# A gated mix of sliding-window attention and a GELU MLP on one core: the account of dense products per score step, weighted by stage

## The chip, the cores and the metric

One core of one Trainium2 chip. The metric is the device time of one launch in microseconds (us), the median of several runs. A profile of one launch goes with it; its span runs from the first to the last instruction on the core. The engines are named as the profile names them: PE (matrix products; PEld is its weight load), DVE (vector engine), ACT (scalar engine), POOL (GpSimd) and SP (the queue that issues the DMAs here).

## The reference, cut to what matters

x is 2048 x 512. Two branches are mixed by a gate per row: attention with 32 heads of width 16 and a causal window of 256, and an MLP of width 1792 with a GELU.

```python
g = _sigmoid((x * gate_w).sum(-1, keepdims=True))
qkv = x @ wqkv                                   # 32 heads of 16
scores = einsum("bhqd,bhkd->bhqk", q, k) * 16 ** -0.5
scores = where(0 <= i - j < 256, scores, -1e9)
a = (softmax(scores) @ v) @ wo
b = _gelu(x @ w1 + b1) @ w2 + b2
return g * a + (1 - g) * b
```

## The kernel before

**Two streams on one engine.** The PE's program is one list, written in order by the kernel itself (a manual schedule). It is made of two streams that are woven together.

The *dense stream* is a generator, `dense()`: the products for q, k and v of four tiles of 512 rows, then eight MLP rounds, then the output product. A round `mlp(n)` works on one tile of 512 rows and one half of the 14 column blocks of the MLP. It has two stages: in stage u (the first product, x @ w1, tiles named `u`) there are 28 *triples*, in stage y (the second product, tiles named `y`) 28 more. A triple is what the helper `mm3` (L107 to L110) issues: three matmuls of 512 columns, since every float32 product is split into high and low parts. The stages are called u0, y0, u1, y1 up to u7, y7 here. After each block of four triples of stage u comes the GELU of its 512 columns: four instructions on ACT and three on DVE (L719 to L737). In u0, u3, u4 and u7 there is extra work: weights are loaded and split there (ACT L178; DVE, or POOL in the early ones, L182).

The *score stream* is attention. A step `u` of the main loop (L941 on) has four turns. In a turn the PE gets up to two score matmuls: `sm` (`att_max`, L519), whose row maxima are wanted twelve steps ahead, and `st` (`att_exp`, L564), whose exponentials are taken. Each `sm` is read by one DVE instruction (L524, tile `jm`) with a small one behind it that reads the accumulator; each `st` is read by one ACT exponential (L586, tile `pt`), after which POOL cuts the window's corners (L580). An `sm` with its `st` is called a *score pair* below. Once in four steps a PV pass (`att_pvs`, L608) multiplies probabilities and values, 96 rows in the profile for most of them. `sm`, `st` and the PV pass share PSUM: there are three buffers with tag "sm" and three with tag "st"; a PV pass takes one of each.

**What sets the weave.** After each turn the loop calls `fill(STEP / 4)`. `fill` adds these 582.5 ns to an account, `owed`, and draws triples from the dense stream until the account is no longer positive; each triple takes its nominal cost `MM3`, 3 x 227 = 681 ns, off it. In stage u the turns are written one by one. In all other stages two turns are joined (`pair`, L951): two score pairs stand next to each other, and then two turns' worth of triples is drawn. The list `stage` tells the loop which stage the dense stream is in.

```python
    def fill(ns):
        owed[0] += ns
        while owed[0] > 0:
            c = next(run)
            if c is None:
                owed[0] = -1e9
            else:
                owed[0] -= c
                tick(c)
```

**The other engines.** `tick(ns)` moves a nominal clock on by what the PE was given. What the other engines do is put on a list with a nominal delay (`after`) and written into their programs when the nominal clock reaches it. So the order on DVE, ACT, POOL and SP follows from the order on the PE; at run time each engine works through its own list in order, and semaphores hold it where data or buffers are not ready.

**Words used below.** In a u stage a score pair stands alone between two triples, or two score pairs follow each other with no triple between: a *double*. In a y stage two score pairs always follow each other, and behind them stand one triple (a *short gap*) or two.

Of the kernel before, what the change touches and what calls it, by code (L numbers as in the profile page):

```python
# [32 lines left out]
def gated_mix(ctx: ExitStack, tc: tile.TileContext, x, wqkv, wo, w1, b1, w2, b2, gate_w, out):  # L33
# [12 lines left out]
    def f32(ap):  # L46
        return ap.bitcast(F32)
# [59 lines left out]
    def mm3(p, lh, ll, rh, rl, first, last):  # L107
        nc.tensor.matmul(p, lh, rh, start=first, stop=False)  # L108
        nc.tensor.matmul(p, lh, rl, start=False, stop=False)  # L109
        nc.tensor.matmul(p, ll, rh, start=False, stop=last)  # L110
# [4 lines left out]
    def after(ns, fn, *args):  # L115
        now[1] += 1
        heapq.heappush(todo, (now[0] + ns, now[1], fn, args))
# [12 lines left out]
    def need(*keys):  # L130
        for key in keys:
            while key not in done:
                step_todo()
# [67 lines left out]
    def load(key):  # L201

        paced[0] = max(now[0], paced[0] + PACE)
        after(paced[0] - now[0], load_now, key)
# [468 lines left out]
    def load_x(t, name):  # L673
        xt = sb.tile([128, NC, 2, T], F32R, tag="xt", bufs=1, name=f"{name}{t}")

        def part(c):
            nc.sync.dma_start(f32(xt[:, c]), XT[t][c])
            if c == NC - 1:
                done.add(name)
        for c in range(NC):  # L680
            after(MXAT * c, part, c)
        xts[t] = xt

    def load_o(t, cs=range(NC)):

        if ("o", t) not in xts:
            if t == 0:
                v = sb.tile([128, NC, 2, T], F32R, tag="xt", bufs=1, name=f"ot{t}")
                xts["o", t] = [v[:, c] for c in range(NC)]
            else:  # L690
                xts["o", t] = {}
        for n, c in enumerate(cs):
            load_part(t, c, LAND0 if t == 0 else LANDO, 700 * n)
# [50 lines left out]
    def ya_load(k):  # L744
        n, b = divmod(k, NB)
        if n == len(TURNS):
            return
        half, t = TURNS[n]
        if half == 0 and k:
            yas[k] = xts["b2"]  # L750
            return
        yas[k] = ya = sb.tile([128, D], F32, tag="ya", bufs=2, name=f"ya{t}_{half}{b}")
        if half == 0:
            xts["b2"] = ya
            nc.sync.dma_start(ya, b2.partition_broadcast(128))
        else:
            need(("y", 0, t, b))
            nc.sync.dma_start(ya, YA[t][slice(b * 128, (b + 1) * 128)])

    def ya_of(k):  # L760
        while k not in yas:
            step_todo()
        return yas.pop(k)
# [3 lines left out]
    def mlp(n):  # L767
        half, t = TURNS[n]
        if n == 0:
            ya_load(0), ya_load(1)  # L770
        last = n % NT == NT - 1
        if n and TURNS[n - 1][1] != t:
            need(f"mx{n - 1}")
        xt = xts[t]
        stage[0] = "u"
        hs = []
        for i in range(HF):
            f = half * HF + i
            need(("w", ("w1", f)))
            w = wt["w1", f]  # L780
            p = ps.tile([128, T], F32, tag="d", bufs=2, name=f"u{t}_{f}")
            for c in range(NC):
                mm3(p, w[:, 0, c], w[:, 1, c], xt[:, c, 0], xt[:, c, 1], c == 0, c == NC - 1)
                yield MM3
            h = sb.tile([128, 2, T], F32R, tag="h", bufs=7, name=f"h{t}_{f}")
            after(100, gelu, p, f, h)
            hs.append(h)
            if last and later:
                load(later.pop(0))
        if n == 0:  # L790
            for c in range(NC):
                nc.sync.dma_start(XT[t][c], f32(xt[:, c]))
        if n + 1 < len(TURNS) and TURNS[n + 1][1] != t:
            load_x(TURNS[n + 1][1], f"mx{n}")
        ps_ = {}

        def y_start(b):
            if n + 1 == len(TURNS) and b == 2:
                load_o(0)
            ps_[b] = ps.tile([128, D], F32, tag="d", bufs=2, name=f"y{t}_{half}{b}")  # L800

        def y_end(b):
            ts = slice(b * 128, (b + 1) * 128)
            if n + 1 < len(TURNS) and b == NB - 1:
                y = f32(sb.tile([128, 2, T], F32R, tag="h", bufs=7, name=f"yo{t}_{half}{b}")[:, 0])
            elif n + 1 < len(TURNS) or b >= 2:
                y = sb.tile([128, D], F32, tag="sq", bufs=2, name=f"yo{t}_{half}{b}")
            else:
                if b == 0:
                    ybs["w"] = sb.tile([128, 2, T], F32, tag="w", bufs=14, name="yo")  # L810
                y = ybs["w"][:, b]
            nc.vector.scalar_tensor_tensor(y, ps_[b], 0.5, ya_of(n * NB + b), op0=ALU.mult, op1=ALU.add)
            after(HOLD, ya_load, n * NB + b + 2)

            def store():
                nc.sync.dma_start((YA, YB)[half][t][ts], y)
                done.add(("y", half, t, b))
            if n + 1 < len(TURNS):
                after(HOLD, store)
            else:  # L820
                ybs[t * NB + b] = y
                done.add(("y", half, t, b))


        stage[0] = "y"
        turns = [(0, i) for i in range(HF - 1)] + [(1, i) for i in range(YSWAP)] + [(0, HF - 1)]
        turns += [(1, i) for i in range(YSWAP, HF)] + [(b, i) for b in range(2, NB) for i in range(HF)]
        for b, i in turns:
            ts = slice(b * 128, (b + 1) * 128)
            if i == 0:  # L830
                y_start(b)
            need(hs[i].name, ("w", ("w2", half * HF + i)))
            w = wt["w2", half * HF + i]
            mm3(ps_[b], hs[i][:, 0, ts], hs[i][:, 1, ts], w[:, 0], w[:, 1], i == 0, i == HF - 1)
            yield MM3
            if last and b == NB - 1 and later:
                load(later.pop(0))
            if i == HF - 1:
                after(100, y_end, b)
# [79 lines left out]
        for t in range(NT):  # L919
            yield from final(t)  # L920

    stage = ["qk"]
    run = dense()
    owed = [0.0]

# [5 lines that stand above are left out]
            if c is None:  # L931
                owed[0] = -1e9
            else:
                owed[0] -= c
                tick(c)

    NU = NG * NKB
# [5 lines left out]
    for u in range(-LEAD, NU):  # L943
# [3 lines left out]
        for i in range(4):  # L947
# [6 lines left out]
            else:  # L954
                pair = (i,)
            for op, i in [(op, k) for k in pair for op in ORDER[:3]] + [("f", k) for k in pair]:
                if op == "s" and u >= 0:
                    att_exp(u // NKB, u % NKB, i)
                if op == "m" and m < NU:
                    att_max(gm, bm, i ^ XOR)  # L960
                if op == "p" and i == PVAT and 1 <= u <= NU - LEAD:
# [40 lines left out]
GELU = (700, 1500, 3600, 4600, 6000, 7000)  # L1002
XAT = 3
ORDER = 'mspf'
XOR = 1
PACE = 4000.0
LAND = 7500.0
# [36 lines left out]
```

## Time and profile before

| | |
|---|---|
| median of 3 runs | 750.57 us (749.57 to 752.2) |
| the profiled execution | 749.65 us |
| its span | 747.9 us |
| granted clock of the PE | 1.00 over the span |
| PE, share of the span busy | 98% |
| DVE, ACT, POOL | 70%, 56%, 50% |

The span is 1.75 us shorter than the time of the execution it belongs to, and that execution is 0.92 us under the median of the three.

In the profile the three matmuls of a triple are the lines L108, L109 and L110. Matmuls are pipelined, and their recorded durations overlap: how fast the PE goes is read from the starts of successive matmuls, and not from the duration of one. "Busy" is the union of the recorded durations. The stages can be found in the trace by their tiles, since each begins with the first matmul of its tile; they lie one behind the other from u0 at 151.3 us to the end of y7 at 697.9 us. Ahead of them come the products for q, k and v, behind them the output product.

### The profile page before, as it was taken

To read this page: it belongs to the slowest core of one execution; us is meant where nothing else is said; L and a number is where in the kernel's file an instruction comes from. 1 tells how busy PE (TensorE), PEld (TensorE's weight loads), DVE (VectorE), ACT (ScalarE), POOL (GpSimd) and SP (SyncE) were. 2 spreads that over 40 slices of the span, in tenths; PEclk is the share of its full clock that TensorE was granted. 3 is DMA by queue.
4 is the path that set the end of the run, shared out by engine and by line. 5 is a ranking of instruction groups with operands and counts; after the bars stand their busy time and mean duration, and the time that the engine had idled before them with its cause. 6 is when DMAs were issued, how large, how long until landed. Compare 5 with 4: busy or idle time off the path is not lost.

```text
span 747.9 us, 17961 instructions
## 1 busy us (share of the span) xinstructions
PE 732.7 (98%) x6129; PEld 604.4 (81%) x6129; DVE 520.1 (70%) x1567; ACT 421.5 (56%) x972; POOL 372.3 (50%) x846
## 2 busy tenths in 40 slices
PE   8999999998999999999999999999999999999998
PEld 7888888876788888888887877888888888867786
DVE  4532325799768867986798689768867986784552
ACT  4434532358537845864695478438745863794550
POOL 4200000339756865876577568747765875630000
PEclk9999999999999999999999999999999999999999
DMA  9889798998895687899575979996799799468572
GB/s 326 319 272 404 261 391 273 291 293 182 270 259 134 162 243 205 175 222 271 146 179 149 242 211 234 249 237 152 178 256 235 194 224 270 136 181 226 191 252 111
DMA packets 179260, 172.12 MB, mean 230 GB/s; under 512 B 56673, under 2 KB 122977, under 8 KB 179169
## 3 DMA queue, kind: packets, MB, share of 16 engines
q1 hardware_dynamic: 179168, 170.97, 81.4%
q8 instruction: 49, 0.80, 0.5%
q14 instruction: 43, 0.34, 0.1%
HBM read 108.53 MB, written 62.39 MB: 229 GB/s over the span
## 4 chain that ended last, share of the span: by engine, by line
PE 85%; DVE 5%; ACT 3%; issue 3%; DMA 2%; SPq 1%; POOL 1%; DVEq 0%; ACTq 0%
PE sm L519 9%; PE st L564 8%; PE pv_sm L608 7%; PE y L108 7%; PE y L109 6%; PE y L110 6%; PE u L108 5%; PE u L109 5%; PE u L110 5%; PE qk L110 4%; PE qk L108 4%; PE qk L109 4%; PE a L108 2%; DVE jm L524 2%; PE v L108 2%
## 5 line engine op out<-in xcount | busy, mean ns | idle before, releaser
L524 DVE CUSTOM_DVE_ANT_0 jm<-sm,mask 128x320 bf16<-128x320 f32 (+4 forms) x512 | 238.1, 465 | 95.3 <-PE sm L519 61.1
L580 POOL TENSOR_SCALAR_AFFINE_SELECT pt<-pt 64x256 f32<-64x256 f32 (+1 forms) x538 | 227.7, 443 | 108.5 <-ACT pt L586 98.1
L586 ACT ACTIVATE pt<-st 128x320 f32<-128x320 f32 (+4 forms) x512 | 199.6, 424 | 139.1 <-PE st L564 136.0
L519 PE MATMUL sm<-kd,qd 96*128 96x320 f32 (+4 forms) x512 | 153.9, 312 | 6.3 <-DVE M L524 5.5
L564 PE MATMUL st<-qs,ks 128*128 128x320 f32 (+4 forms) x512 | 153.9, 309 | 1.9 <-ACT pt L586 1.9
L546 POOL CAST qs<-tt 4x256 fp32r<-4x256 f32 x256 | 124.6, 487 | 53.3 <-DVE tt L539 42.7
L519 PEld LDWEIGHTS sm<-kd,qd 96*128 96x128 f32 x512 | 96.3, 188 | 33.2 <-DVE M L524 13.7
L564 PEld LDWEIGHTS st<-qs,ks 128*128 128x128 f32 x512 | 97.1, 190 | 18.8 <-ACT pt L586 3.2
L108 PE MATMUL y<-w,h 128*128 128x512 f32 x224 | 88.5, 395 | 0.0
L109 PE MATMUL y<-w,h 128*128 128x512 f32 x224 | 87.9, 393 | 0.0
L110 PE MATMUL y<-w,h 128*128 128x512 f32 x224 | 87.9, 392 | 0.0
L108 PE MATMUL u<-mx,w 128*128 128x512 f32 x196 | 80.0, 408 | 0.0
L109 PE MATMUL u<-mx,w 128*128 128x512 f32 x196 | 77.4, 395 | 0.0
L110 PE MATMUL u<-mx,w 128*128 128x512 f32 x196 | 77.1, 393 | 0.0
L608 PE MATMUL pv_sm<-pt,vbuf 64*32 64x320 f32 (+4 forms) x1408 | 73.6, 346 | 0.2
L608 PE MATMUL pv_st<-pt,vbuf 64*32 64x320 f32 (+4 forms) x1408 | 73.3, 346 | 0.0
L608 PEld LDWEIGHTS pv_sm<-pt,vbuf 64*32 64x32 f32 x1408 | 50.2, 106 | 20.2 <-issue 2.4
L325 DVE TENSOR_TENSOR qke<-qk,qke 128x512 fp32r<-128x512 f32 x32 | 22.0, 688 | 46.9 <-ACT qke L322 33.2
L322 ACT ACTIVATE qke<-qk 128x512 fp32r<-128x512 f32 x32 | 19.1, 597 | 56.2 <-PE qk L110 32.5
L110 PEld LDWEIGHTS y<-w,h 128*128 128x128 f32 x224 | 42.0, 188 | 9.8
L338 POOL MEMSET vx<- 128x32 f32 x16 | 2.4, 156 | 89.0 <-DMA SQ<-qke 44.5
L608 PEld LDWEIGHTS pv_st<-pt,vbuf 64*32 64x32 f32 x1408 | 46.1, 106 | 0.0
(148 smaller groups left out, 1332.7 us busy)
## 6 DMA issues: line engine op xcount, KB each, us to landing
kd<-SK SPq DMA_DIRECT2D x32, 384.0 KB
qs<-SQ SPq DMA_DIRECT2D x64, 192.0 KB
mx<-XT SPq DMA_DIRECT2D x24, 512.0 KB
SQ<-qke SPq DMA_DIRECT2D x16, 512.0 KB
SK<-qke SPq DMA_DIRECT2D x16, 512.0 KB
ND<-nd SPq DMA_DIRECT2D x32, 256.0 KB
raw_w<-in_B_w_dram SPq DMA_DIRECT2D x28, 256.0 KB
ks<-SK SPq DMA_DIRECT2D x32, 192.0 KB
```

The lines of the kernel that those rows point to most:

```text
L108: nc.tensor.matmul(p, lh, rh, start=first, stop=False)
L109: nc.tensor.matmul(p, lh, rl, start=False, stop=False)
L110: nc.tensor.matmul(p, ll, rh, start=False, stop=last)
L322: nc.scalar.activation(e[:, h], p, AF.Copy)
L325: nc.vector.tensor_sub(e[:, 1 - h], p, f32(e[:, h]))
L519: nc.tensor.matmul(p[:, :w], qd[0:96, n, pr, 128 * j:128 * (j + 1)], kd[0:96, n, pr, k1 - w:k1], start=True, stop=True)
L524: nc.vector.tensor_tensor_reduce(junk[:, :w], p[:, :w], mask[:, 320 - w:320], 1.0, -3e38, ALU.add, ALU.max, M[:, 2 * (b % RB) + hb, pr:pr ...
L546: nc.gpsimd.tensor_copy(dst, src.unsqueeze(1).broadcast_to([4, 2, RB, 32]))
L564: nc.tensor.matmul(p[:, :w], ks[:, slot(g_, kb // NB), pr, at:at + 128], qs[:, pr, k0:k0 + w], start=True, stop=True)
L580: nc.gpsimd.affine_select(out=v, in_=v, pattern=[[0, v.shape[1]], [1 - 2 * e, 64]], compare_op=ALU.is_ge, fill=0.0, base=-e, channel_multi ...
L586: nc.scalar.activation(pt[:, hf, pr, :w], p[:, :w], AF.Exp, scale=SCALE)
L608: nc.tensor.matmul(pv[r // 64][32 * i:32 * i + 32, q - c * T:e - c * T], vts[g_, b // NB][r:r + 64, v:v + 32], rhs(r), start=start, stop=s ...
```

## The change

The account of `fill` no longer takes off the nominal cost of a triple but that cost times a weight of the stage. The nominal clock still advances by the plain cost.

```diff
-        stage[0] = "u"
+        stage[:] = "u", DUE["u"][n]
...
-        stage[0] = "y"
+        stage[:] = "y", DUE["y"][n]
...
-    stage = ["qk"]
+    stage = ["qk", 1.0]
...
-                owed[0] -= c
+                owed[0] -= c * stage[1]
                 tick(c)
...
+DUE = {'u': (0.88, 1.0, 1.0, 0.9, 0.9, 1.0, 1.0, 0.86),
+       'y': (1.04, 1.08, 1.06, 1.02, 1.06, 1.04, 1.0, 1.14)}
```

A weight under 1 lets more triples be drawn per turn, so that fewer scores stand in that stage; a weight over 1 the other way round. The sum of the deviations is -0.46 over the u stages and +0.44 over the y stages. No instruction is added or taken away: all 512 `sm`, 512 `st`, all triples and all PV passes stay, and PE's program has the same number of rows before and after. What the weave looks like, counted in the two programs (sm / st in the stage; doubles in u stages, short gaps in y stages):

| stage | weight | sm / st before | now | doubles or short gaps before | now |
|---|---|---|---|---|---|
| u0 | 0.88 | 31 / 21 | 27 / 17 | 3 | 0 |
| y0 | 1.04 | 33 / 33 | 35 / 35 | 7 | 6 |
| u1 | 1.0 | 33 / 33 | 32 / 32 | 5 | 4 |
| y1 | 1.08 | 33 / 33 | 36 / 36 | 6 | 8 |
| u2 | 1.0 | 32 / 32 | 32 / 32 | 4 | 4 |
| y2 | 1.06 | 34 / 34 | 36 / 36 | 6 | 8 |
| u3 | 0.9 | 32 / 32 | 28 / 28 | 4 | 1 |
| y3 | 1.02 | 32 / 32 | 34 / 34 | 5 | 7 |
| u4 | 0.9 | 33 / 33 | 29 / 29 | 5 | 1 |
| y4 | 1.06 | 33 / 33 | 35 / 35 | 7 | 9 |
| u5 | 1.0 | 33 / 33 | 33 / 33 | 4 | 4 |
| y5 | 1.04 | 33 / 33 | 35 / 35 | 6 | 8 |
| u6 | 1.0 | 32 / 32 | 31 / 31 | 5 | 4 |
| y6 | 1.0 | 34 / 34 | 33 / 33 | 6 | 5 |
| u7 | 0.86 | 16 / 32 | 18 / 28 | 2 | 0 |
| y7 | 1.14 | 0 / 32 | 0 / 38 | 6 | 10 |

The one PV pass of u0 stands in y0 now. Attention ends at the same place in both programs, at the end of y7, with one PV pass left that stands in the output product.

Three places on the PE, before and now. A name such as `sm_12_0` is block 12, turn 0 of the score stream, `u_3` the fourth column block of stage u; the number behind it is a running one.

In u0, around the first exponential of the second turn, before:

```order
L519 MATMUL sm_12_0_1789<-kd,qd 128x320
L564 MATMUL st_0_1_1794<-qs,ks 128x320
L519 MATMUL sm_12_3_1797<-kd,qd 128x320
L564 MATMUL st_0_2_1802<-qs,ks 128x320
L108 MATMUL u_3_1807<-xt_1009,w_3_1480 128x512
L109 MATMUL u_3_1807<-xt_1009,w_3_1480 128x512
L110 MATMUL u_3_1807<-xt_1009,w_3_1480 128x512
```

and now:

```order
L519 MATMUL sm_12_0_1801<-kd,qd 128x320
L564 MATMUL st_0_1_1805<-qs,ks 128x320
L108 MATMUL u_3_1782<-xt_1009,w_3_1480 128x512
L109 MATMUL u_3_1782<-xt_1009,w_3_1480 128x512
L110 MATMUL u_3_1782<-xt_1009,w_3_1480 128x512
L519 MATMUL sm_12_3_1816<-kd,qd 128x320
L564 MATMUL st_0_2_1819<-qs,ks 128x320
```

The double is gone: a triple stands between the two score pairs.

In y4, behind its first PV pass, before:

```order
L564 MATMUL st_8_3_6923<-qs,ks 128x320
L108 MATMUL y_11_6846<-w_8_6225,h_8_6322 128x512
L109 MATMUL y_11_6846<-w_8_6225,h_8_6322 128x512
L110 MATMUL y_11_6846<-w_8_6225,h_8_6322 128x512
L108 MATMUL y_11_6846<-w_9_6354,h_9_6392 128x512
L109 MATMUL y_11_6846<-w_9_6354,h_9_6392 128x512
L110 MATMUL y_11_6846<-w_9_6354,h_9_6392 128x512
L519 MATMUL sm_5_1_6945<-kd,qd 128x320
```

and now:

```order
L564 MATMUL st_8_3_6933<-qs,ks 128x320
L108 MATMUL y_11_6822<-w_10_6405,h_10_6447 128x512
L109 MATMUL y_11_6822<-w_10_6405,h_10_6447 128x512
L110 MATMUL y_11_6822<-w_10_6405,h_10_6447 128x512
L519 MATMUL sm_5_1_6952<-kd,qd 128x320
L564 MATMUL st_9_0_6957<-qs,ks 128x320
L519 MATMUL sm_5_0_6961<-kd,qd 128x320
L564 MATMUL st_9_1_6965<-qs,ks 128x320
```

A gap of two triples has become a short one.

At the head of y7, where no `sm` is left, before:

```order
L564 MATMUL st_8_0_10114<-qs,ks 128x320
L564 MATMUL st_8_1_10117<-qs,ks 128x320
L108 MATMUL y_10_10101<-w_8_6225,h_8_9763 128x512
L109 MATMUL y_10_10101<-w_8_6225,h_8_9763 128x512
L110 MATMUL y_10_10101<-w_8_6225,h_8_9763 128x512
L108 MATMUL y_10_10101<-w_9_6354,h_9_9842 128x512
L109 MATMUL y_10_10101<-w_9_6354,h_9_9842 128x512
L110 MATMUL y_10_10101<-w_9_6354,h_9_9842 128x512
L564 MATMUL st_8_2_10132<-qs,ks 128x320
L564 MATMUL st_8_3_10134<-qs,ks 128x320
```

and now, behind the same first triple of y7:

```order
L564 MATMUL st_6_2_10089<-qs,ks 128x320
L564 MATMUL st_6_3_10092<-qs,ks 128x320
L108 MATMUL y_10_10078<-w_8_6215,h_8_9751 128x512
L109 MATMUL y_10_10078<-w_8_6215,h_8_9751 128x512
L110 MATMUL y_10_10078<-w_8_6215,h_8_9751 128x512
L564 MATMUL st_7_0_10103<-qs,ks 128x320
L564 MATMUL st_7_1_10105<-qs,ks 128x320
```

Here too the gap between the first two bursts is one triple instead of two, and the stage begins six `st` further back in the score stream.

## The prediction

> **What bounds the kernel now.** The first page comes first. It gives the PE nearly the whole span:
>
> ```profile
> PE 732.7 (98%) x6129; PEld 604.4 (81%) x6129; DVE 520.1 (70%) x1567; ACT 421.5 (56%) x972; POOL 372.3 (50%) x846
> ```
>
> The change takes nothing off the PE, so all that it can win is time in which the PE waits. The view of waits for the PE, and the entry of its weight load in the view for all engines, say for whom:
>
> ```profile
> PE sm L519 <- DVE M L524: 5.5, 11, 1.0
> PE st L564 <- ACT pt L586: 1.9, 3, 1.2
> ...
> PEld sm L519 <- DVE M L524: 13.7, 27, 1.2
> ```
>
> In the overlapped part the PE waits for the row maxima of DVE, a little for ACT, and never for a DMA. The 70% of DVE is a mean over unlike stages, so the third view is the table of busy times by stage. Its columns: from:to, length, then PE, PEld, DVE, ACT, POOL busy, each with its number of rows, clock, DMA share, GB/s. The rows are u0, y0, u1, y1 and so on to y7.
>
> ```profile
> 151.30:185.60 34.30, 31.44 (x210) 24.36 (x209) 31.71 (x94) 25.12 (x52) 21.81 (x38) 1.00 0.95 225
> 185.60:221.10 35.50, 34.54 (x344) 28.71 (x344) 24.62 (x84) 17.02 (x42) 24.36 (x63) 1.00 0.97 271
> 221.10:254.90 33.80, 33.74 (x320) 28.66 (x319) 28.51 (x92) 25.25 (x57) 23.86 (x51) 1.00 0.59 136
> 254.90:289.20 34.30, 34.30 (x344) 28.74 (x344) 23.80 (x84) 16.18 (x40) 23.23 (x60) 1.00 0.89 244
> 289.20:322.30 33.10, 33.10 (x317) 27.84 (x317) 28.19 (x90) 25.50 (x58) 23.25 (x50) 1.00 0.77 169
> 322.30:357.60 35.30, 35.29 (x347) 29.35 (x346) 25.95 (x90) 17.02 (x42) 23.51 (x62) 1.00 0.96 259
> 357.60:391.90 34.30, 33.64 (x317) 27.90 (x317) 30.24 (x92) 27.16 (x62) 22.90 (x47) 1.00 0.65 160
> 391.90:427.60 35.70, 34.48 (x342) 28.45 (x341) 27.16 (x91) 18.27 (x44) 25.31 (x61) 1.00 0.73 184
> 427.60:463.70 36.10, 35.04 (x319) 27.95 (x318) 32.43 (x97) 28.47 (x64) 24.71 (x48) 1.00 0.86 223
> 463.70:499.20 35.50, 34.77 (x344) 28.46 (x343) 26.06 (x90) 16.86 (x42) 23.70 (x60) 1.00 1.00 255
> 499.20:533.20 34.00, 33.79 (x319) 28.21 (x318) 26.85 (x89) 25.49 (x57) 22.68 (x50) 1.00 0.60 150
> 533.20:567.30 34.10, 34.10 (x344) 28.55 (x343) 25.17 (x87) 16.32 (x41) 23.50 (x58) 1.00 1.00 247
> 567.30:600.70 33.40, 33.40 (x319) 28.18 (x318) 28.44 (x93) 25.76 (x58) 23.93 (x51) 1.00 0.83 206
> 600.70:635.40 34.70, 34.57 (x347) 29.19 (x345) 25.10 (x87) 16.16 (x42) 23.64 (x58) 1.00 1.00 255
> 635.40:667.40 32.00, 31.88 (x302) 25.74 (x302) 26.34 (x69) 25.77 (x60) 19.21 (x38) 1.00 0.51 138
> 667.40:697.90 30.50, 29.30 (x309) 23.06 (x309) 17.51 (x37) 19.03 (x49) 0.00 (x0) 1.00 0.72 214
> ```
>
> Stages with the same PE content serve as twins. u4 and u5 hold the same matmuls (x319), but u4 takes 36.1 us and u5 34.0: 2.1 more. u3 is 1.05 over the mean of u2 and u6 (34.3 against 33.25). y0 and y4 are each 1.3 over the mean of y1 and y5 (34.2), y2 0.6 over y6. DVE explains the order: it is busy 92%, 88% and 90% of u0, u3 and u4, and 79 to 85% of the other four u stages ahead of u7, which run without much waiting. For u0 and y3, whose content differs, the pace of the PE is needed:
>
> ```profile
> 364.30 0.40 PE L108 MATMUL u<-mx,w 128*128 128x512 f32 x1
> ...
> 365.00 0.31 PE L519 MATMUL sm<-kd,qd 96*128 96x320 f32 x1
> 365.15 0.31 PE L564 MATMUL st<-qs,ks 128*128 128x320 f32 x1
> 365.30 0.39 PE L108 MATMUL u<-mx,w 128*128 128x512 f32 x1
> ...
> 366.39 0.24 PE L608 MATMUL pv_sm<-pt,vbuf 64*32 64x64 f32 x1
> ...
> 368.71 0.50 PE L108 MATMUL u<-mx,w 128*128 128x512 f32 x1
> ```
>
> From start to start a triple takes 0.70 us, a score matmul 0.15, so a score pair 0.30; a PV pass takes 2.3. u0 has one PV pass and 14 score matmuls fewer than u5: 34.0 - 2.3 - 2.1 = 29.6, and it takes 34.3, so 4.7 over. y3 has a pair less than y1 and y5: 33.9, and takes 35.7, 1.8 over. The sum over u0, u3, u4, y0, y2, y3, y4 is 4.7 + 1.05 + 2.1 + 1.3 + 0.6 + 1.8 + 1.3 = 12.85 us. That is the ceiling of what an even load could bring in these stages.
>
> **The change part by part.** The sum is made against the profiled execution, 749.65 us.
>
> *Term 1, fewer pairs in u0, u3, u4.* Each loses four pairs (the counts stand in the table of the change). What one takes off DVE:
>
> ```profile
> 165.08 0.48 DVE L524 CUSTOM_DVE_ANT_0 jm<-sm,mask 128x320 bf16<-128x320 f32 x1
> ...
> 165.49 0.68 DVE L731 SCALAR_TENSOR_TENSOR x1h<-sqh,x1h 128x512 f32<-128x512 f32 x1
> ...
> 158.09 0.49 DVE L524 CUSTOM_DVE_ANT_0 jm<-sm,mask 128x320 bf16<-128x320 f32 x1
> ...
> 158.74 0.49 DVE L524 CUSTOM_DVE_ANT_0 jm<-sm,mask 128x320 bf16<-128x320 f32 x1
> ```
>
> A maximum with another kind of instruction behind it holds DVE for 0.41 us (165.08 to 165.49); one with a maximum behind it 0.65. Where DVE sets the pace the stage gets 0.41 shorter per pair; the pair costs 0.30 on the PE in the y stage to which it goes. Twelve pairs at 0.11: -1.3 us. Bounds: +3.6 if the u stage frees nothing and the y stage pays in full, -4.9 if the y stage takes them in free time. I take DVE's price in the u stage and the PE's in the y stage, since DVE is at 88 to 92% in the ones, and y1, y5 and y6 show the PE busy for nearly all their length.
>
> *Term 2, the doubles.* u0, u3 and u4 lose ten (3, 3, 4). One of u0:
>
> ```profile
> 161.52 0.31 PE L519 MATMUL sm<-kd,qd 96*128 96x320 f32 x1
> 161.67 0.31 PE L564 MATMUL st<-qs,ks 128*128 128x320 f32 x1
> 162.65 0.41 PE L519 MATMUL sm<-kd,qd 96*128 96x320 f32 x1 [0.67 <-DVE M L524]
> ```
>
> The second `sm` of the double starts 0.98 us behind the `st` where the pace is 0.15: it finds no free PSUM buffer. The bounds of one double are 0 (u2 and u6 have four and five, and hardly wait) and this 0.83. I take what two maxima in a row cost DVE more than two apart, 0.65 - 0.41 = 0.24: the two of a double come to DVE at the same time and tend to stand together there. Ten make -2.4 us, bounds 0 and -8.3 (no more than the 7.85 that u0, u3 and u4 are over).
>
> *Term 3, what the u stage leaves to the y stage.* y0, y3 and y4 are 4.4 us over though DVE is at 69 to 76% there, and their longest wait stands near the head:
>
> ```profile
> 188.62 0.31 PE L564 MATMUL st<-qs,ks 128*128 128x320 f32 x1
> 189.89 0.41 PE L519 MATMUL sm<-kd,qd 96*128 96x320 f32 x1 [0.96 <-DVE M L524]
> ```
>
> It lies 3 us into y0, while DVE still works off the GELU of the last block of u0. I take half of the 4.4, -2.2, since the arrears are made smaller and not removed; bounds 0 and -4.4.
>
> *Term 4, more pairs in the y stages.* Of their pairs the PE time is in term 1. What is new is the short gap: the wait of 0.96 stands behind one. Over y0 to y6 there are 51 instead of 43. Bounds: 0 (y1 has six, and the PE is busy for 34.30 of its 34.30) and 8 x 0.96 = +7.7. I take one in ten of the full price, +0.8, nearer to y1 since DVE stays under 80% in these stages.
>
> *Term 5, the head of y7.* The longest wait for ACT:
>
> ```profile
> 670.01 0.30 PE L564 MATMUL st<-qs,ks 128*128 128x320 f32 x1
> 671.51 0.41 PE L564 MATMUL st<-qs,ks 128*128 128x320 f32 x1 [1.21 <-ACT pt L586]
> ```
>
> Now a triple fewer (0.70 us) stands ahead of the second burst, while ACT has the same GELU instructions to do: the wait grows by 0.7. Bounds 0 (u7 gives ACT four exponentials fewer) and 1.4 for two lost triples. +0.7.
>
> *At nothing:* the DMAs are as many as before and only move past each other on SP: in u0 a weight load now stands ahead of the loads of `kd` and `qd` for the next block, and what SP holds back is later by one load. No PE wait in the list ends with a DMA, so this is hidden by what is loaded ahead. The lone PV pass of u0 goes to y0 as one PE block of the same length. If the DMA's cover went, in y4 to y6 (DMA share 1.00), the next `sm` would be late, at a price that no row here gives. `u7` gives up pairs for which DVE was no limit (82%): nothing.
>
> The sum: -1.3 - 2.4 - 2.2 + 0.8 + 0.7 = -4.4, so 745.25 us in the profiled execution. With the 0.92 by which it was under the median of the three: 746.2 us, 0.6% less. About 0.3%, 2.25 us, is what a measurement of this kernel can tell from no change.
>
> **The rivals.**
>
> *The load goes along (no change).* A pair that leaves a u stage takes its DVE time and its PE time with it. The share of DVE against PE work in u4 goes from 32.43 / 34.0 = 95% to (32.43 - 4 x 0.41) / (34.0 - 4 x 0.30) = 94%: hardly less crowded. Then only term 1 holds, and terms 4 and 5 give it back: -1.3 + 1.5 = +0.2, 750.8 us. For it: this quotient. Against it: the doubles' waits stand in the trace.
>
> *The short gaps bind (slower).* Place: the y stages, where two bursts with one triple between them put four maxima on DVE within 4 x 0.30 + 0.70 = 1.9 us, while DVE takes 4 x 0.41 to 4 x 0.65 = 1.6 to 2.6. If each of the eight new short gaps ends as at 188.62, that costs 7.7, with y7 8.4; against it stand 3.7 from terms 1 and 2, and nothing from term 3, since new arrears come up: 750.57 + 4.7 = 755.3 us. It decides from 0.65 us per new gap, at which terms 1 to 3 and 5 are used up (5.2 / 8). For it: the place of the wait in y0. Against it: y1 and y5.
>
> *u0 is held by something else.* Two long instructions stand side by side there, on DVE and on POOL:
>
> ```profile
> 160.49 1.69 DVE L725 SCALAR_TENSOR_TENSOR sqh<-sqh,x1h 128x512 f32<-128x512 f32 x1
> ...
> 160.01 1.62 POOL L182 TENSOR_TENSOR w<-raw_w,w 128x512 fp32r<-128x512 f32 x1 [6.76 <-ACT w L178]
> ```
>
> DVE's instruction is of the kind and shapes that take 0.68 at 165.49 above; here it takes 1.69, and it ends 0.55 after POOL's: DVE has stood still behind POOL, and the wait at 162.65 follows. POOL splits a weight in u0 only, and still does so after the change. If u0's waits come from this, u0 keeps its 4.7: terms 1 and 2 lose a third (0.4 and 0.7), term 3 what y0 gives (0.65). The sum is then -2.6: 747.9 us. [...]
>
> *More than the sum.* If nearly all waits in the three u stages and their y stages go, -9 us of the ceiling: 741.6.
>
> **How the numbers follow.** The forecast (743.5 to 748.3) has 0.46, the u0 rival 0.10 (its 747.9 lies at the edge of the band: 0.06 below it, 0.04 within), more than the sum 0.06, no change 0.19, slower 0.19. So faster by over 0.3% is 0.46 + 0.06 + 0.06 = 0.58, within it 0.19 + 0.04 = 0.23, slower 0.19. The range is from 741.5 (most of the ceiling) to 753.0 (the short gaps at seven tenths of their price, +5.4 and +0.7, against -3.7: 2.4 over 750.57); outside lie most of the slower case and a few per cent below, together under 0.2. The likeliest's own range is 743.5 to 748.3.
>
> **What would show it.** In the table by stage of the changed kernel: u0, u3 and u4 with DVE still busy over 85%, but the PE within 1 us of the length, and the waits of `sm` for DVE (5.5 us on the PE, 13.7 on its weight load) down by a third or more. Term 3 is right if the wait 3 us into y0 is shorter than 0.96 or gone. Term 4 is wrong if new waits of `sm` stand behind short gaps in y1, y2, y4 or y5, and these stages are longer than their pairs explain (0.30 each). Term 5 is wrong if `st` waits less than 1.2 us at the head of y7. The rival of u0 is right if long DVE instructions beside POOL's splits still have waits of `sm` behind them. The prediction fails as a whole if the sum of the waits is the same and has only moved from u to y.

## The result, and the profile after

| | before | after |
|---|---|---|
| median of 6 runs each | 750.74 us (749.57 to 752.2) | 755.93 us (755.38 to 758.6) |
| ratio to before, 95% interval | | 1.0078 [1.0058, 1.0097] |
| the profiled execution, its span | 749.65, 747.9 us | 757.34, 755.6 us |
| mean granted clock of the PE | 1.000 | 0.995 |

The change makes the kernel 5.2 us slower, and the time lies outside the predicted range (741.5 to 753.0). The profiled executions are 7.7 us apart; the one of after is 1.4 us over its median. The first line of its page shows nearly the shares of before (PE 98%, DVE 69% instead of 70%, ACT 56%). The view of waits for the PE (engine and line, what it waited for: us in all, times, longest):

```profile
PE sm L519 <- DVE M L524: 4.8, 8, 1.0
PE a L110 <- DVE ot L709: 4.0, 2, 3.2
PE st L564 <- ACT pt L586: 3.0, 6, 1.0
...
PE a L108 <- ACT ot L706: 0.8, 1, 0.8
```

The waits of the score stream are hardly changed (`sm` 5.5 before, `st` 1.9). New are two rows of tile `a`, the output product, in which the PE waits for `ot`. The table by stage of after (columns as in the prediction; the last row is the output product), and the output product of before:

```profile
151.40:181.90 30.50, 28.12 (x129) 21.68 (x128) 28.12 (x76) 22.00 (x45) 17.01 (x29) 1.00 0.98 278
181.90:219.50 37.60, 37.48 (x420) 30.80 (x420) 26.16 (x96) 18.80 (x46) 26.62 (x68) 1.00 0.95 246
219.50:252.70 33.20, 33.20 (x318) 27.98 (x317) 29.15 (x91) 25.88 (x58) 22.89 (x48) 1.00 0.53 131
252.70:288.30 35.60, 35.37 (x350) 29.57 (x350) 25.29 (x90) 17.30 (x43) 24.28 (x65) 1.00 0.91 232
288.30:321.40 33.10, 33.10 (x318) 27.88 (x318) 28.87 (x92) 25.51 (x58) 23.31 (x49) 1.00 0.82 189
321.40:356.90 35.50, 35.33 (x349) 29.47 (x349) 25.54 (x92) 17.34 (x44) 25.45 (x63) 1.00 0.95 250
356.90:390.00 33.10, 32.67 (x310) 26.69 (x309) 28.35 (x83) 26.11 (x58) 22.06 (x43) 1.00 0.68 162
390.00:426.50 36.50, 35.74 (x346) 29.04 (x345) 28.41 (x96) 18.95 (x46) 25.76 (x63) 1.00 0.77 192
426.50:460.90 34.40, 33.59 (x312) 26.97 (x311) 30.80 (x88) 26.45 (x59) 22.42 (x43) 1.00 0.86 217
460.90:497.50 36.60, 35.58 (x348) 29.23 (x347) 27.03 (x95) 18.40 (x45) 26.55 (x66) 1.00 1.02 260
497.50:531.00 33.50, 33.50 (x320) 28.26 (x319) 27.41 (x89) 25.47 (x57) 23.28 (x50) 1.00 0.60 143
531.00:565.80 34.80, 34.80 (x348) 29.09 (x347) 25.51 (x92) 16.96 (x43) 23.50 (x61) 1.00 1.00 241
565.80:599.70 33.90, 33.31 (x317) 27.77 (x316) 28.95 (x91) 25.49 (x57) 23.55 (x50) 1.00 0.84 211
599.70:634.20 34.50, 34.47 (x345) 28.97 (x344) 25.39 (x87) 16.75 (x42) 23.22 (x59) 1.00 1.04 268
634.20:665.00 30.80, 30.80 (x300) 25.56 (x299) 25.80 (x70) 24.48 (x54) 20.14 (x40) 1.00 0.38 105
665.00:696.95 31.95, 29.97 (x315) 23.80 (x315) 17.40 (x38) 20.03 (x52) 0.00 (x0) 1.00 0.77 217
696.95:755.60 58.65, 50.53 (x301) 39.92 (x301) 23.97 (x39) 18.09 (x31) 0.00 (x0) 0.94 0.51 173
```

```profile
697.90:747.90 50.00, 46.69 (x301) 38.01 (x299) 23.15 (x38) 17.17 (x29) 0.00 (x0) 1.00 0.56 191
```

From u0 to y7 the changed kernel takes 545.55 us instead of 546.60: it gains 1.05. The output product takes 58.65 instead of 50.00 with the same 301 matmuls: 8.65 lost. The difference is the 7.7 of the spans, so **in these two executions the whole loss lies behind the stages that the change weights.** The PE in that place, in order of time (the bracket is the idle time ahead of the row and what ended it), and the busy time in two stretches behind the waits (the last three columns are clock, DMA share, GB/s):

```profile
713.52 0.50 PE L108 MATMUL a<-wo,ot 128*128 128x512 f32 x1 [0.81 <-ACT ot L706]
...
717.41 0.79 PE L110 MATMUL a<-wo,ot 128*128 128x512 f32 x1 [3.16 <-DVE ot L709]
718.01 0.63 PE L108 MATMUL a<-wo,ot 128*128 128x512 f32 x1
718.43 0.63 PE L109 MATMUL a<-wo,ot 128*128 128x512 f32 x1
...
723.77 0.39 PE L110 MATMUL a<-wo,ot 128*128 128x512 f32 x1
```

```profile
717.40:723.50 6.10, 6.08 (x14) 4.79 (x15) 3.08 (x6) 1.17 (x2) 0.00 (x0) 0.50 0.61 185
723.50:730.00 6.50, 6.50 (x30) 5.34 (x29) 2.39 (x4) 2.00 (x4) 0.00 (x0) 1.00 0.81 276
```

The PE waits 0.81 and 3.16 us, and then works 14 matmuls at half clock: 0.43 from start to start instead of 0.23, 2.8 us more. With the waits of the list (4.0 + 0.8) that makes 7.6 of the 8.65.

What it waits for is the end of attention. For each tile of 512 rows the last group of heads goes through a **chain of round trips through DRAM**, all issued by SP in order: the result of the PV pass is stored (`nd` to ND, L636), its denominators are loaded (`den`, L646), DVE takes the reciprocal (L650), it is stored (L653), numerator and reciprocals are loaded (`num`, `rb`, L658), multiplied (L662) and stored (OT, L665), and the piece is loaded again as `ot` (L703), whose high part ACT makes (L706) and whose low part DVE (L709). DVE at that time, after and before:

```profile
716.46 0.35 DVE L650 RECIPROCAL den<-den 128x32 f32<-128x32 f32 x1 [4.93 <-DMA den<-ND]
716.73 1.22 DVE L709 TENSOR_TENSOR ot<-ot 128x512 fp32r<-128x512 f32 x2
```

```profile
712.97 0.35 DVE L650 RECIPROCAL den<-den 128x32 f32<-128x32 f32 x1 [0.69 <-DMA den<-ND]
```

The low part for which the PE stood was behind a reciprocal on DVE, and this waited for a 16 KB load. ACT works through its list in order too, and so the chain stopped the PE once already inside y7. Of the 3.0 us that the PE waits for `st`, 0.98 fall on the last score matmul of y7, whose buffer comes free by an exponential that stands on ACT behind a wait for an `ot` load. The PE and ACT of the changed kernel:

```profile
696.82 0.30 PE L564 MATMUL st<-qs,ks 128*128 128x64 f32 x1 [0.98 <-ACT pt L586]
```

```profile
695.46 1.15 ACT L706 ACTIVATE ot<-ot 128x512 fp32r<-128x512 f32 x2 [0.97 <-DMA ot<-OT]
```

The SP queue ahead of DVE's reciprocal, after and before:

```profile
707.34 0.58 SPq L658 DMA_DIRECT2D rb<-RD  x1
708.03 1.82 SPq L703 DMA_DIRECT2D ot<-OT  x4
...
710.36 0.59 SPq L646 DMA_DIRECT2D den<-ND  x1
```

```profile
703.31 0.32 SPq L703 DMA_DIRECT2D ot<-OT  x1
...
705.55 1.49 SPq L703 DMA_DIRECT2D ot<-OT  x3
...
710.23 0.59 SPq L646 DMA_DIRECT2D den<-ND  x1
```

Before, a single piece goes out at 703.31 and three more two us later. After, it stands behind the `rb` load, which waits for a store, and leaves with the three others at 708.03; the small load comes right behind these four and an output store of 256 KB, and takes 6.1 us to its reciprocal, where before it took 2.7. Further up the chain, the store from which the awaited piece comes is late too. It is that of the second tile of 512 rows, behind the third-last PV pass, and its data are ready at the same time (DVE's last step on `nd` starts at 676.36 before and at 676.41 after). SP before and after:

```profile
677.08 0.34 SPq L636 DMA_DIRECT2D ND<-nd  x1
```

```profile
676.42 4.06 SPq L848 DMA_DIRECT2D kd<-YB  x1
680.59 0.41 SPq L636 DMA_DIRECT2D ND<-nd  x1
```

From this store to the first matmul of the output product there were 697.9 - 677.1 = 20.8 us before; now there are 697.0 - 680.6 = 16.4. Of the 4.4 us of this *cover*, 3.5 went on SP, and 0.95 because y7 ends earlier.

### The profile page after: what moved, and what is told of

Same layout as the page of the kernel before. It is cut to its first block, busy times and chain, and to the rows that moved or that the text cites. A ratio compares the mean times of both kernels' runs of the same rounds, so it can differ in the third digit from the quotient of the medians.

```text
span 755.6 us, 17961 instructions
## 1 busy us (share of the span) xinstructions
PE 737.3 (98%) x6129; PEld 606.5 (80%) x6129; DVE 521.0 (69%) x1567; ACT 423.4 (56%) x972; POOL 372.9 (49%) x846
## 4 chain that ended last, share of the span: by engine, by line
PE 82%; DMA 8%; DVE 3%; ACT 2%; SPq 2%; issue 2%; POOL 0%; DVEq 0%; ACTq 0%; POOLq 0%
PE sm L519 9%; PE st L564 8%; PE pv_sm L608 7%; PE y L108 6%; PE y L109 6%; PE y L110 6%; PE u L108 6%; PE u L109 5%; PE u L110 5%; PE qk L110 4%; PE qk L108 4%; PE qk L109 4%; PE v L108 2%; PE v L110 2%; PE v L109 2%
## 5 line engine op out<-in xcount | busy, mean ns | idle before, releaser
L519 PEld LDWEIGHTS sm<-kd,qd 96*128 96x128 f32 x512 | 96.3, 188 | 32.3 <-DVE M L524 12.8
L109 PE MATMUL y<-w,h 128*128 128x512 f32 x224 | 88.0, 393 | 0.0
L109 PE MATMUL u<-mx,w 128*128 128x512 f32 x196 | 77.3, 395 | 0.0
L725 DVE SCALAR_TENSOR_TENSOR sqh<-sqh,x1h 128x512 f32<-128x512 f32 x56 | 44.1, 788 | 2.1 <-ACT sqh L722 1.6
```

What stands on the lines that cost most here:

```text
L519: nc.tensor.matmul(p[:, :w], qd[0:96, n, pr, 128 * j:128 * (j + 1)], kd[0:96, n, pr, k1 - w:k1], start=True, stop=True)
L725: nc.vector.scalar_tensor_tensor(sq, sq, GC, x1, op0=ALU.add, op1=ALU.mult)
```

## The experiments

The expectations name theories by letters. **A:** the loss is made in the output product by an order on DVE: the reciprocal of den3_3 (the denominators of row tile 3) stands ahead of the low part of ot1_3 (the last piece of row tile 1, the second tile). **B:** the short gaps of the y stages. **C:** the chain has too little time between the last PV passes and the output product, wherever it is then felt. **D:** the half clock. **E:** any other order of this program is worse. F and G come with the order on SP. All are the changed kernel with the edit shown, unless the kernel before is named. Each ratio is to the kernel before on the same chip.

**Which weights.**

```diff
 e1: -'u': (..., 0.86), 'y': (..., 1.14)
     +'u': (..., 1.0),  'y': (..., 1.0)
 e2: +'u': (1.0,) * 7 + (0.86,), 'y': (1.0,) * 7 + (1.14,)
```

> The change with the weights of u7 and y7 put back to 1.0. Theory A (the loss is made in the output product: the weights of the last round bring the low part of the last piece of tile 1, ot1_3, behind the reciprocal den3_3 on DVE): here ot1_3 stands ahead of den3_3 again, the output product takes 50 us as before, and the time is 749 to 750.5 us. Theory B (the new short gaps in the y stages cost what the rival said): six of the eight y stages keep their new weights, so the time stays at 753 us or more.

> Kernel before, with the weights of u7 (0.86) and y7 (1.14) alone. Theory A: den3_3 stands ahead of ot1_3 on DVE, as in the change, and most of the loss is there: 755 to 758 us, with a PE wait of about 3 us in the output product. Theory B: one y stage of eight is denser, so no more than 1.5 us are lost: under 752.5 us.

Without the weights of the last round: 753.43 us, 1.0039 [1.0026, 1.0052]. With these alone: 760.92, 1.0140 [1.0123, 1.0157]. The last round does the greater harm, but the other weights also cost 0.4%, and the two parts don't add up to the whole (3.2 and 10.7 against 5.2 us). In e1 the waits stand at other places of the output product:

```profile
PE a L108 <- ACT ot L706: 2.5, 1, 2.5
PE a L108 <- DVE ao L879: 2.4, 2, 2.3
```

**The order on DVE, and the clock.** e3 puts the low part ahead of the reciprocal. e5, e6 and e7 give the reciprocals of the last group a later place on DVE, e6 in the kernel before, e7 in e1's. e4 puts 50 matmuls that nobody reads ahead of the waiting triple.

```diff
 e3: -REACH = 2500.0
     +REACH = 500.0
 e5, e6, e7: -DIVS = (..., (4500, 5700, 8500, 17000, 18500))
             +DIVS = (..., (5690, 5700, 8500, 17000, 18500))
 e4, at (t, b, c) == (1, 0, NC - 1):
     +for _ in range(50):
     +    nc.tensor.matmul(keep[:, 0:192], mask[:, 64:192], mask[:, 64:256], start=True, stop=True)
```

> The change as it is, with the nominal delay between the store of a normalised piece and its being loadable (REACH) at 500 ns and not 2500. All weights stay. ot1_3 now stands ahead of den3_3 on DVE. Theory A: 749 to 750.5 us, the output product back near 50 us. Theory C (the piece itself lands too late, since attention of the last group ends later relative to the dense products; the order on DVE matters little): a PE wait of 1 to 3 us stays in the output product, 752 to 754 us.

> The change, with one nominal delay altered: the reciprocal of a last piece's denominators (den, L650) is written 1.19 us of the nominal clock later, just ahead of its store. On DVE the low parts of ot1_3 and ot2_0 now stand ahead of den3_3; the other engines' programs stay. Theory A (what stops the PE in the output product is that DVE waits, in order, at den3_3 for a DMA, and the low part of ot1_3 behind it): the wait of 3.2 us and the half clock behind it go, 750 to 751.5 us. Theory C (the piece itself lands too late): 754 us or more, since only the place of the wait moves.

> The kernel before with the same altered delay, as a control. Both theories: within 1 us of before (749.5 to 751.5 us), since DVE waited 0.7 us at den3_3 and the PE not at all.

> The change without the weights of u7 and y7, with the same altered delay. Of the two waits of that kernel in the output product, the first (2.4 us, for a PSUM buffer that an addition on DVE behind den3_3 would free) goes by theory A; the second (2.5 us, for a piece whose load is behind three others on SP) stays: 750.5 to 751.5 us. Theory C: 753 to 754 us.

> The change, with 50 matmuls of zeros (192 columns, 0.08 us each, 4 us in all) put on the PE ahead of the triple that waits in the output product; their result is not read. Theory D (the six microseconds at half clock behind the wait come from the PE standing idle): the clock stays at 1.00 there, and the time falls by about 2.8 us, to 753 us. Rival (the low clock there has another cause): the clock still falls to 0.50 for some 6 us, and the time stays at 755.5 to 757 us.

| | median us | ratio [95%] | waits of the PE for `a` in the profile |
|---|---|---|---|
| e3 | 758.85 | 1.0115 [1.0100, 1.0130] | 4.1 for DVE `ao` |
| e5 | 758.81 | 1.0086 [1.0054, 1.0117] | 3.3 for ACT `ot`, 1.2 for DVE `ao` |
| e7 | 758.22 | 1.0096 [1.0062, 1.0131] | 4.0 for ACT `ot`, 2.2 for DVE `ao` |
| e6 | 751.61 | 1.0011 [0.9997, 1.0024] | |
| e4 | 756.41 | 1.0089 [1.0065, 1.0113] | 1.5 for ACT `ot` |

A falls: with that order changed the PE waits elsewhere, and as long. In e3 the additions `ao` now stand behind the same reciprocal, which waits longer than in the changed kernel:

```profile
721.42 0.35 DVE L650 RECIPROCAL den<-den 128x32 f32<-128x32 f32 x1 [5.76 <-DMA den<-ND]
```

In e5 and e7, where it stands later, the longest wait is one for ACT. The table holds only tile `a`. e3, e5 and e7 lose another 2.9, 2.1 and 2.2 us ahead of it, in y7, where `st` waits for ACT and ACT for a DMA of the chain (3.7, 2.1 and 6.5 us). The edit of e5 costs the kernel before nothing that can be told (e6). D is only a part: in e4 the clock stays at 1.00 in the stretch that ran at half,

```profile
711.20:717.40 6.20, 6.20 (x60) 5.41 (x59) 1.40 (x4) 4.01 (x7) 0.00 (x0) 1.00 0.73 236
717.40:723.50 6.10, 6.10 (x28) 5.04 (x28) 3.80 (x7) 0.97 (x2) 0.00 (x0) 1.00 0.62 195
```

but the median is that of the changed kernel (the profiled execution is 2.2 us shorter); the pieces don't come earlier, and the PE waits 1.5 us for a later one, though the 50 unread matmuls keep it busy ahead of that for about 4 of the 6.20 us in the first of these rows (60 matmuls; the other ten at 0.23 take 2.3).

**The splits on POOL in u0** (kernel before, all early splits on POOL), a test of the rival of u0:

```diff
-after(LAND + 1500, split, key, nc.gpsimd if key[1] % 2 else nc.vector)
+after(LAND + 1500, split, key, nc.gpsimd)
```

> The kernel before with the early weight splits all on POOL and none on DVE (four moved in u0). If the sheer load of DVE sets the pace of u0, DVE loses about 3 us of work there and u0 gets shorter than 33 us (34.3 before). If u0 is held by DVE standing still behind POOL's splits, with more of them u0 stays at 34 us or gets longer, with more DVE instructions of 1.3 us and over.

A single execution, 753.35 us. u0 takes 35.66 instead of 34.30, but the `sm` waits there are 1.9 us as before (2.0), and 179.6 to 183.2 went at a clock of 0.54, which alone costs about 3.6 x 0.46 = 1.7. Nor did it take load off DVE, which is busy for 30.8 us of u0 instead of 31.7. So it doesn't show whether the splits hold u0. The collisions themselves are there, three instead of two: each time DVE ends 0.55 us behind POOL (POOL from 166.42 for 1.27, DVE from 166.89 for 1.35).

**More time for the chain.** A smaller STEP draws fewer triples per score step in every stage, so that attention ends earlier against the dense stream. Counted in the programs, behind the third-last and second-last PV pass there are 23 and 10 triples up to the output product before, 20 and 8 after, 23 and 9 in e1.

```diff
-STEP = 2330.0
+STEP = 2310.0     e10: 2290.0
```

> The change, with STEP at 2310 and not 2330 ns: slightly fewer dense products per score step everywhere, so that attention ends earlier against the dense stream. From the second-to-last PV passes to the first triple of the output product there are 23 and 11 triples (before 23 and 10, the change 20 and 8). Theory C (the normalisation of the last group, a chain of DMA round trips, has too little time until the output product needs its pieces): the waits there go back to under 1 us and the clock stays at 1.00, 749 to 751 us. Theory E (it is the exact order on SP and DVE that was good before, and any other order is worse): 753 us or more.

> The change with STEP at 2290: 26 and 14 triples. Theory C: no waits in the output product, but the woven part has more scores per triple; 749 to 751.5 us. Theory E: 753 us or more.

> The change without the weights of u7 and y7, with STEP at 2310: 26 and 13 triples (without the new STEP 23 and 9, 753.4 us). Theory C: the two waits of 2.4 and 2.5 us go, 748.5 to 750.5 us. Theory E: 753 us or more.

> The kernel before with STEP at 2310, as a control: 27 and 13 triples. Theory C: there is no wait to win, within 1.5 us of before. Theory E: any other order is worse, 753 us or more.

| | triples behind the PV passes | median us of 10 runs | ratio [95%] |
|---|---|---|---|
| e9: after, 2310 | 23 / 11 | 750.27 | 0.9995 [0.9984, 1.0005] |
| e10: after, 2290 | 26 / 14 | 750.50 | 1.0000 [0.9981, 1.0019] |
| e11: e1, 2310 | 26 / 13 | 750.47 | 0.9993 [0.9975, 1.0012] |
| e12: before, 2310 | 27 / 13 | 750.82 | 1.0004 [0.9995, 1.0013] |

With all weights kept, the loss is gone, and it goes where it was made. In e9 the last PV pass (2.3 us) stands ahead of the output product and not in it; with it the output product takes 47.7 + 2.3 = 50.0 us, as before. Without it u0 to y7 take 546.4 us (before 546.6, changed kernel 545.55). The output product of e9, the one wait of the PE in it, and the last reciprocal on DVE, which no longer waits:

```profile
699.90:747.60 47.70, 44.27 (x212) 36.65 (x204) 21.56 (x33) 17.05 (x28) 0.00 (x0) 0.99 0.59 199
```

```profile
738.51 0.50 PE L108 MATMUL a<-wo,ot 128*128 128x512 f32 x1 [0.23 <-DVE ao L879]
```

```profile
709.72 0.35 DVE L650 RECIPROCAL den<-den 128x32 f32<-128x32 f32 x1
```

The same can be read in the cover defined above, from the profiled execution of each kernel. The *work in it* is the cover less what the PE waited in it and, in e9 to e12, less the last PV pass, which in all other kernels stands behind the first matmul of the output product. The last column holds the waits of the PE for `a` in the output product, but for the 0.2 that every kernel has.

| | cover, us | work in it, us | waits behind it, us |
|---|---|---|---|
| e10 | 25.4 | 23.1 | 1.8 |
| e12 | 25.2 | 22.9 | 0 |
| e11 | 25.1 | 22.8 | 0 |
| e9 | 23.2 | 20.8 | 0 |
| before, e6, e14 | 20.8 | 20.8 | 0 |
| e8 | 20.8 | 20.8 | 0.5 |
| e18 | 20.8 | 20.8 | 2.9 |
| e1 | 19.5 | 19.5 | 4.7 |
| e15 | 20.1 | 18.9 | 3.2 |
| e17 | 19.6 | 18.9 | 3.1 |
| e13 | 18.7 | 18.7 | 3.2 |
| e3 | 21.2 | 18.3 | 3.9 |
| e7 | 20.5 | 18.2 | 6.0 |
| e2 | 18.5 | 18.1 | 4.7 |
| e4 | 17.6 | 16.6 | 1.5 (behind the unread matmuls) |
| e16 | 17.4 | 16.4 | 3.4 |
| after | 16.4 | 15.4 | 4.8 |
| e5 | 16.4 | 13.4 | 4.2 |

All eleven kernels with less than 20 us of work have waits of 1.5 us or more; of the nine with 20.8 or more, six have none. How long the waits are doesn't follow the work (4.2 us at 13.4 in e5, 6.0 at 18.2 in e7). Two don't fit in well, e18 (see below) and e10, whose profiled execution took 756.16 us (1.3 us of wait for ACT `ao` and 0.5 for `ot`); two of e10's ten executions took over 755 us, which is left unexplained. Otherwise it is C that the runs show, and B and E fall: e9 keeps the weights of all the y stages, and four other orders cost nothing at the median. They also show what the weights are worth without the damage: nothing that can be measured (with the same STEP, e9 0.9995 and e12 1.0004).

**The order on SP.** Two more theories. **F:** the chain becomes late on SP, by the `kd` issue in front of the store. **G:** the small `den` load comes late because it stands behind 1 MB of `ot` loads. e13 swaps the store and the `kd` load of 4.06 us, e14 does the opposite in the kernel before. e15 adds to e13 an earlier OT store, so that a lone `ot` piece passes the `num` and `rb` loads. e16 puts the last `den` load ahead of three `ot` loads; e17 is e13 and e16; e18 is e16's edit in the kernel before.

```diff
 e13: -after(1500 + YGAP * k, load_y, *divmod(k, 2))
      +after(1500 + YGAP * k + (k >= 4) * 1000, load_y, *divmod(k, 2))      e14: - (k >= 4) * 1000
 e15: +DIVS = (..., (4500, 5700, 8500, 16500, 17500))
 e16: -after(NORM if g_ * NT + c < NQ - 4 else 3500, att_norm, c, g_ // 2)
      +after(NORM if g_ * NT + c < NQ - 4 else 3500 if c < NC - 1 else 1500, att_norm, c, g_ // 2)
```

> The changed kernel with one swap on SP alone: the first of the last four ND stores goes ahead of the first kd load instead of behind it (the order of all other engines stays). In the changed kernel this kd issue held SP for 4.06 us (676.42 to 680.48), while nd was ready at 677.10. Theory F (the chain becomes late on SP, by that issue in front of the store): the ND store is issued near 677.2 instead of 680.6, the chain runs some 3 us earlier, the waits in the output product (0.8 + 3.2 + 1.0) fall under 2 us without half clock, and the time is 750.5 to 753. Theory C alone (the chain has too little time against the dense stream, and this issue is an accident of one execution or is only moved): the ot pieces stay late, 754.5 to 757.

> The kernel before with the same swap the other way round: the kd load ahead of the ND store. Theory F: the kd issue takes 2 to 4 us in front of the store, the chain gets later by that, and the kernel is slower than before by 1 to 5 us, with waits of a for ot in the output product. Theory C alone: the kernel before has the slack for it (10 triples between the second-last PV pass and the output product), no change within 0.15%.

> The swap of e13, and the nominal delays of the last group's product and OT store shortened from 17000 and 18500 to 16500 and 17500, so that the load of the fourth piece of the third-last tile stands ahead of the num and rb loads of the next on SP, which wait for a reciprocal's store. Theory C with an in-order SP: the piece for which the output product waited at 713.52 and 717.41 no longer stands behind the wait for RD, both waits go, and the time is that of the kernel before or up to 1 us under it (749.5 to 751.5), without any change of STEP. If only more time for attention helps: 754 to 757.

> The changed kernel, with the last den load moved ahead of three ot loads on SP (the nominal delay of the last group's last normalisation is 1500 instead of 3500). In the changed kernel this load of 16 KB is issued at 710.36, right behind four ot loads of 256 KB, and its reciprocal starts at 716.46: 6.1 us; in the kernel before it is issued 3.2 us behind three such loads and takes 2.7 us. Theory G (the small load stands in the DMA queues behind 1 MB, and DVE stands behind it in order): reciprocal within 4 us of the issue, the wait of 3.16 us for ot's low part falls under 1.5 us, no half clock, time 751.5 to 754. Theory C alone (every link of the chain is late, this one is not special): the waits move to another ot or to the d buffers, 754.5 to 757.5.

> The edits of e13 and e16 together. If the two places on SP make up the loss (theories F and G): no wait over 1 us in the output product, 750 to 752, and the weights' own worth appears, at most 1 us under the kernel before. If the lack of time of the chain is general (theory C): 753 to 756.

> Control: the kernel before with the edit of e16. Theories C and G: its chain has slack there, so no change within 0.2%, 749.5 to 752; if the edit itself costs (SP standing longer for the ND store ahead of the ot loads): 753 or more.

| | median us | ratio [95%] |
|---|---|---|
| e13 | 754.84 | 1.0053 [1.0039, 1.0067] |
| e15 | 753.63 | 1.0041 [1.0025, 1.0057] |
| e16 | 755.02 | 1.0057 [1.0045, 1.0069] |
| e17 | 753.86 | 1.0050 [1.0037, 1.0063] |
| e14 (before) | 750.60 | 0.9997 [0.9983, 1.0011] |
| e18 (before) | 750.69 | 1.0008 [0.9993, 1.0023] |

By their middle values these edits give back 0.2 to 0.4% of the 0.8, and none the whole; of their intervals only that of e15 lies wholly below that of the changed kernel. In e13 the store goes out at 678.07, 2.5 us earlier than in the changed kernel, but its own issue then holds SP for 1.83 us, and the cover grows to 18.7 only. e16 does what G says to the link that it touches (the reciprocal 4.1 us behind the issue at 709.42, the wait of the PE 1.06 instead of 3.16), and then the PE waits at the last piece:

```profile
715.07 0.50 PE L110 MATMUL a<-wo,ot 128*128 128x512 f32 x1 [1.06 <-DVE ot L709]
728.12 0.65 PE L108 MATMUL a<-wo,ot 128*128 128x512 f32 x1 [2.30 <-ACT ot L706]
```

So F and G name two links of a chain that is late in all of them. e14 and e18 leave the kernel before as it is at the median. The `kd` issue ahead of the store took only 0.65 us in e14, so this control doesn't test a hold of 4 us. And the kernel before stands near the edge: of its own executions 4 of 96 took 753.7 us or more, of e18's three of twelve, and the profiled one of these, 755.12 at a cover of 20.8, has the same kind of waits:

```profile
716.96 0.50 PE L108 MATMUL a<-wo,ot 128*128 128x512 f32 x1 [1.22 <-DVE ao L879]
729.31 0.50 PE L108 MATMUL a<-wo,ot 128*128 128x512 f32 x1 [1.64 <-ACT ot L706]
```

No kernel tried was measurably faster than the one before.

## Why the prediction was wrong

**The step that failed** is the one headed "At nothing": "the DMAs are as many as before and only move past each other on SP", and "No PE wait in the list ends with a DMA, so this is hidden by what is loaded ahead". That holds for weights and blocks, which are loaded ahead: in the changed kernel's list, too, no wait of the PE ends with a DMA. It doesn't hold for the chain at the end of attention, each link of which waits for the one before. What was put at nothing took 4.8 us of waits in the output product, 2.8 us more by the half clock behind them, and about 1 us at the end of y7. The list of waits couldn't show it: in the kernel before the PE had no such wait yet, and where it has one, the list names the last engine ahead of the PE (DVE `ot`, ACT `ot`) and not the DMA behind that engine. The sum ended with y7, and the output product was taken as unchanged. The last PV pass does stand at the same place in both programs, as was said of the end of attention, but the two passes ahead of it don't: 23 and 10 triples stood between them and the output product, and 20 and 8 do now. What counts is the cover: how much dense work stands behind the last PV passes, and what stands ahead of each link on SP. Before, 20.8 us were just enough; the change left 16.4 (15.4 of work), and e9, with as much work as before, brings the time back. None of the rivals was right: the slower one forecast 755.3, near the median, but by waits in the y stages that did not come. That its number is near is luck.

**The terms.** A round's two stages together, net of the pairs that moved in from other rounds or out to them (0.30 us each; they cancel over all rounds):

| round | 0 | 1 | 2 | 3 | 4 | 5 | 6 | 7 | sum |
|---|---|---|---|---|---|---|---|---|---|
| change of length, us | -1.70 | +0.70 | +0.20 | -0.40 | -0.60 | +0.20 | +0.30 | +0.25 | -1.05 |
| pairs | -2 | +2 | +2 | -2 | -2 | +2 | -2 | +2 | 0 |
| what is left, us | -1.10 | +0.10 | -0.40 | +0.20 | 0.00 | -0.40 | +0.90 | -0.35 | -1.05 |

- Term 1 (-1.3) and term 2 (-2.4): rounds 3 and 4 show nothing of them. The ten doubles went, but the waits stayed: over the kernel those of `sm` fell from 5.5 to 4.8 us on the PE and from 13.7 to 12.8 on its weight load, where a third or more had been forecast. In u0, from 145 us to the end of the stage, before and after:

```profile
PE sm L519 <- DVE M L524: 2.0, 4, 0.7
```

```profile
PE sm L519 <- DVE M L524: 1.9, 4, 0.7
```

A wait behind a double was taken for the double's price. DVE is busy for 92% of u0 in both kernels, and the next `sm` now waits behind a triple (0.71 us at 168.22, 0.56 at 176.84).
- Term 3 (-2.2): only round 0 gained, 1.1. The wait of 0.96 us at the head of y0 is gone, as the forecast asked, but one of 1.02 now stands 4.4 us into y4 (at 465.34).
- Term 4 (+0.8): rounds 1, 2 and 5, each with two more short gaps, are +0.1, -0.4 and -0.4. They cost nothing.
- Term 5 (+0.7): the longest wait of `st` is 1.0 instead of 1.2, and round 7 is at -0.35. It didn't come in the changed kernel. In e9, with the same weights, this wait is 2.13 us (e12, the kernel before at the same STEP: 1.12), so the mechanism isn't refuted.

So for the weave "the load goes along" was the nearest: worked out at +0.2, measured -1.05 in the profile, and without the late chain e9's 0.9995. The rival of u0 had its outcome: u0 has two PV passes and 22 score matmuls fewer than u5 now, 33.5 - 4.6 - 3.3 = 25.6, and takes 30.5, 4.9 over, where it was 4.7. Whether POOL's splits are the cause is open after e8.

**Open** is also why the issue of the same `kd` load holds SP between 0.65 us (e9) and 5.46 (e5), and that of the store itself for 3.94 us in e6 and 0.34 before, and with that why executions of one kernel differ by up to 7 us when the chain is tight (e7: 755.23 to 762.19).

## What to carry to other kernels

Before a change that shifts work between stages, follow the chain that the last stage waits for through its DMAs, and measure how much work on the main engine covers it: here 20.8 us of work were enough in most kernels, and less than 20 in none. A list of waits of the main engine names only the last releaser; look up what that releaser waited for, above all with several tensors going through DRAM on one queue. And a wait that stands behind a pattern is not yet the price of the pattern: here the patterns went and the waits stayed.

## What the runs showed of the hardware

**The clock fell in the output product of every kernel that had a wait of 2.85 us or more there, and of one with 2.30.** After 3.16 us (changed kernel) it was 0.50 for 6.1 us; after 3.9 (e2) 0.50 over the next 4.9; after 3.16 (e15) 0.64 over the next 4.7; after 2.85 (e13) 0.59 over the next 3.15; after 2.30 (e16) 0.56 over the next 3.9. e3, e5 and e7, whose longest waits there were 3.9, 3.3 and 4.0, had a mean clock of 0.995 over the execution. In these eight kernels the longest matmul of L109 in tile `a` took 0.63 us, as in the stretch at half clock above; in the twelve others 0.40, with waits of up to 2.5 (in e1 the clock stayed at 1.00 behind 2.5 and 2.3). At the end of y7, behind 2.1 us for `st` (e5), the first three matmuls of the output product started 0.5 us apart (0.3 and 0.2 in the changed kernel); behind 2.13 us for `st` in y7 (e9), matmuls went on at 0.23 from start to start. In e8 it fell to 0.54 with no wait of the PE over 0.65 us in the 7 us before:

```profile
178.00:179.60 1.60, 1.13 (x5) 0.68 (x5) 1.46 (x6) 1.60 (x5) 1.49 (x4) 0.96 0.70 254
179.60:183.20 3.60, 3.60 (x17) 2.86 (x21) 3.40 (x11) 2.64 (x6) 3.39 (x8) 0.54 0.95 233
```

**A small load took longer with more ahead of it:** 16 KB, 6.1 us from issue to use right behind four loads and a store of 256 KB each, 2.7 where 3.2 us lay between them and it, 4.1 right behind one such load, with three more issued after it (e16).
